# A two-branch kernel on one core: its state-space branch regrouped into units of 64 channels, with other buffers, queues and last steps

## The chip, the core and the metric

The kernel runs on one core of a Trainium2 chip. The core has five engines, each with its own in-order instruction stream: TensorE (PE in the profile, with its weight loads as PEld), VectorE (DVE), ScalarE (ACT), GpSimd (POOL) and SyncE (SP). SP, ACT and POOL issue the transfers between the chip's memory and the on-chip buffers. An instruction that waits holds up everything behind it on its own engine. The metric is the time of one execution in microseconds; lower is better.

## What is computed

Two independent branches, joined along the last axis. Branch A is a Fourier mixing layer, a chain of dense float32 products. Branch B is a state-space layer: a convolution of u with a kernel K of length 2048 for each of 512 channels, where K is a sum over 128 complex exponentials.

```python
# A: x is 1 x 2048 x 512
a = einsum("bsd,ed->bse", x, dft_hid_re); b = einsum("bsd,ed->bse", x, dft_hid_im)
yA = einsum("ts,bse->bte", dft_seq_re, a) - einsum("ts,bse->bte", dft_seq_im, b)
# B: u is 1 x 2048 x 512
A = -exp(log_A_real) + 1j * A_imag;  C = (C_real + 1j * C_imag) * dt;  dt = exp(log_dt)
K = 2 * einsum("dn,dnl->dl", C, exp(A * dt * l)).real            # l = 0..2047
yB = irfft(rfft(u, 4096) * rfft(K, 4096))[:2048] + u * D_skip
out = concatenate([yA, yB], axis=-1)
```

## The kernel before

**The stream (branch A, class Fnet).** Each float32 operand is split into a high part (ACT, L192) and a remainder (DVE, L196, the "split"), and each product becomes three matmuls of 128 x 128 by 128 x 512 (L309). There are 160 rounds of 12 such matmuls, 1920 in all. First eight groups of 16 rounds multiply by the sequence matrices and store intermediate tiles p; then four groups of 8 rounds load p again and give the output ya. Operands come through SP into 4 buffers named raw and 3 pairs named hi and lo; results leave through ACT (L323) into y and through SP.

**The state-space part (branch B, class Ssm).** It runs on the same engines, woven into the stream.
- *Tables.* For chunks of 32 channels, DVE builds two tables of exponentials, t1 and t2, by repeated doubling (prod L541, t L550, L564, L570). ACT makes the seeds (L585 to L603) and squares.
- *Taps.* PE multiplies the two tables of a chunk (L738, one "taps" group per chunk, 16 in all), ACT copies the result to ks. After two chunks (64 channels) a first transform of K runs on PE (L768), ACT evicts it to xk_sb (L779), and POOL stores it to xk in memory (L785).
- *Spectrum of u.* u is loaded in eight pieces (L808, by POOL), transformed (L814), evicted (L824) and stored to xu (L831, by POOL), early in the run.
- *Products.* The spectra are loaded (L878, by POOL) in the units "quarter h of 128 channels, part q of 8 values of s", 4 x 4 products. For each, PE makes a second transform of u and of K (64 matmuls, L907), ACT evicts (L918), DVE multiplies complex numbers in ten operations (L929 to L945), PE makes the first inverse transform (L952), ACT evicts to z (L967), and POOL stores z to zs (L973).
- *Second inverse.* Two steps per quarter load zl from zs (L1000, or L1008 for the last quarter, each part on its own), run 32 matmuls (L1023), and send yb out (L1041 by POOL; L1034 by SP and ACT for the last quarter).

**What sets the order.** The order on every engine is fixed when the program is built. The class Plan keeps a list of ready processes and, at each step, takes the one that can start first on its engine, with an estimate of each operation's length (functions act, dve, load, and fixed figures for PE). A process yields an engine with an estimate and an urgency, or a semaphore (a buffer), or an event. So an estimate does not delay anything on the chip, but it decides in which order the instructions stand. The stream's matmuls have the lowest urgency and fill PE wherever the state-space part is not ready. A first inverse (L952) is joined to the next taps group on PE while taps are left.

**Buffers.** A pool b_two serves the first three quarters with single buffers: one xt_u, one xt_k, one uk, one z, one zl. Beside it lies a pool b_tab with everything of the tables, and with ks and xk_sb. When the last xk has been sent, b_tab is given back and b_last takes its place for the last quarter, with more buffers (xt_k 4, uk 3, z 2). The last quarter's u goes into buffers of b_two that are then idle (L858 to L866).

The functions that the change touches, and their callers, as they stand before:

Of the kernel before, what the change touches and what calls it, by code (L numbers as in the profile page):

```python
# [8 lines left out]
F32 = mybir.dt.float32  # L9
# [8 lines left out]
PART = DM // 4  # L18
# [6 lines left out]
def fft_constants():  # L25
# [27 lines left out]
    ib = np.tile(ib.reshape(4, 8, 2, 32, 32).swapaxes(0, 1).reshape(64, 32, 32), (2, 1, 1))  # L53
# [3 lines left out]
HOP, RESULT, LATENCY = 0.3, 0.15, 3.3  # L57
STREAM = 5
URGENT = (lambda: -0.5),
APART = None, True  # L60
# [14 lines left out]
class Plan:  # L75
# [11 lines left out]
    def step(self, p, value):  # L87
        self.now = p[0]
        while True:
# [15 lines left out]
            else:  # L105
                if r[0] != p[5]:
                    p[0] += HOP
                elif r[0] == "dve" and len(r) < 4:
                    p[0] += RESULT
# [27 lines left out]
    def run(self):  # L137

        while self.ready:
# [10 lines left out]
            p[0] = start + dur + (LATENCY if engine.startswith("dma") else 0.0)  # L150
# [184 lines left out]
class Buffers:  # L335


    def __init__(self, pool, n):
        self.pool, self.n, self.un, self.zn = pool, n, UKS[n - 1], ZS[n - 1]
        self.xts, self.uks, self.zbs = {"u": Sem(n), "k": Sem(n * n)}, Sem(self.un), Sem(self.zn)  # L340
# [21 lines left out]
class Ssm:  # L362


    def __init__(self, tc, ctx, plan, nd, ldt, dsk, uG, f1u, f1k, w2, ia, ib, out):
# [6 lines left out]
        self.xk = dram.tile([4, 2, 32, 2, 32, PART], F32, name="xk")  # L372
        self.zs = dram.tile([4, 2, 8, 4, 2, 32, PART], F32, name="zs")
# [12 lines left out]
        self.zq_ev = [Event() for _ in range(4)]  # L386
        self.xk_ev, self.zs_ev = [Event() for _ in range(4)], [Event() for _ in range(4)]
# [5 lines left out]
    def start(self, pool, done):  # L393
        self.tab, self.tab_ev = pool, done
# [6 lines left out]
        self.quarters()  # L401
# [11 lines left out]
    def banks(self, n):  # L413

        yield self.one
# [36 lines left out]
    def load_tables(self):  # L452
# [7 lines left out]
        par = self.tab.tile([128, 32, 64], F32, name="xk_sb").rearrange("p a b -> p (a b)")  # L460
# [65 lines left out]
    def load_par(self, ck):  # L526
# [4 lines left out]
        yield "dma", load(2 * CHUNK)  # L531
# [173 lines left out]
    def kernels(self):  # L705
        for n in range(8):
            yield self.kss
            ks = self.tab.tile([128, 16, 64], F32, name="ks")
# [11 lines left out]
    def taps(self, ks, n, done):  # L720
# [21 lines left out]
        self.taps_left -= 1  # L742
        if other:
            self.plan.set(other)
# [11 lines left out]
    def stage1_k(self, ks, n, ev):  # L756
# [17 lines left out]
        xs = self.tab.tile([128, 32, 64], F32, name="xk_sb")  # L774
# [6 lines left out]
        xk = self.xk[n // 2].rearrange("b l c s d -> b (c s) l d")[..., 64 * (n % 2):64 * (n % 2) + 64]  # L781
        yield "dma", load(1400)
# [4 lines left out]
        if n % 2:  # L787
            self.plan.set(self.xk_ev[n // 2])
        if n == 7:
            self.plan.set(self.tab_ev)  # L790

    def spectrum_u(self):
# [5 lines left out]
        self.xu_sb, self.xus = b.pool.tile([128, 2, 2, DM], F32, name="zl", bufs=b.n), Sem(2)  # L798
        for k in range(8):
            name = "uk"[k % 2]  # L800
            yield self.sets[0].xts[name]
            self.plan.spawn(self.stage1_u(k, name), 1)

    def stage1_u(self, k, name):
        nc, b = self.nc, self.sets[0]
        u = b.pool.tile([128, 2, DM], F32, name=f"xt_{name}")
        yield "dma", load(512)
        nc.gpsimd.dma_start(u, self.uG[:, 2 * k:2 * k + 2])  # L808
# [7 lines left out]
        self.plan.put(b.xts[name])  # L816
# [11 lines left out]
    def store_u(self, x, m, sem):  # L828
        yield "dma", load(512)
# [9 lines left out]
    def quarters(self):  # L839
# [3 lines left out]
        self.left, self.xt = [4] * 4, {}  # L843
        self.xt_ev = {(n, h, q): Event() for n in "uk" for h in range(4) for q in range(4)}
        xu = [self.xu[..., PART * h:PART * h + PART] for h in range(4)]
        self.plan.spawn(self.spectra("u", xu, [self.xu_ev] * 4), 1)
        self.plan.spawn(self.spectra("k", self.xk, self.xk_ev), 1)
        self.plan.spawn(self.products(), 1)
        for h in range(4):
            self.plan.spawn(self.inverses(h), 1)  # L850
# [270 lines left out]
```

## Time and profile before

| what | value |
|---|---|
| three runs | 609.29, 605.38, 608.88 us; median 608.88 |
| profiled execution | 606.6 us |
| its span, first to last instruction | 604.5 us |
| mean granted PE clock | 0.985 |
| memory traffic | 81.56 MB read, 42.73 MB written, 206 GB/s over the span |
| transfers issued by POOL | 58.47 MB, 35.1% of the 16 DMA engines' time |
| transfers issued by SP | 65.33 MB, 33.6% |

The profile has several views. The page gives busy time per engine and the span in 40 slices of 15.1 us, each digit being tenths of busy time. Windows give busy time of each engine in a stretch of the span, in the order PE, PEld, DVE, ACT, POOL (number of instructions in brackets), then the granted clock, the mean share of the DMA engines and GB/s. The chain that ended last is a list of start, length, engine, tile and line, followed back from the last instruction. A row of waits says which engine's instruction waited for what, the sum in us, how many times and the longest. A row of groups gives line, engine, operation, operands, count, then busy us and mean ns of one, then idle time ahead of it and what ended that. The order of instructions is taken from the built programs and has no times. PE executes each float32 matmul of the state-space part as two instructions, so that 64 matmuls of the order are x128 in the trace.

### The profile page before, as it was taken

To read this page: it belongs to the slowest core of one execution; us is meant where nothing else is said; L and a number is where in the kernel's file an instruction comes from. 1 tells how busy PE (TensorE), PEld (TensorE's weight loads), DVE (VectorE), ACT (ScalarE), POOL (GpSimd) and SP (SyncE) were. 2 spreads that over 40 slices of the span, in tenths; PEclk is the share of its full clock that TensorE was granted. 3 is DMA by queue.
4 is the path that set the end of the run, shared out by engine and by line. 5 is a ranking of instruction groups with operands and counts; after the bars stand their busy time and mean duration, and the time that the engine had idled before them with its cause. 6 is when DMAs were issued, how large, how long until landed. Compare 5 with 4: busy or idle time off the path is not lost.

```text
span 604.5 us, 17668 instructions
## 1 busy us (share of the span) xinstructions
PE 573.6 (95%) x7302; PEld 441.6 (73%) x7302; DVE 536.1 (89%) x948; ACT 380.7 (63%) x743; POOL 125.0 (21%) x186
## 2 busy tenths in 40 slices
PE   6999999999979999999999899999999999999962
PEld 4877677787758877876887778867877777776742
DVE  5999889999979999999999999999999999629620
ACT  4589896867846686558565849495945555435430
POOL 0022333110210131022121222013211312330330
PEclk8999999999999999999999999999999999999986
DMA  8999998463573277536776775367877795897775
GB/s 280 299 288 311 327 324 253 159 159 93 145 232 91 89 210 189 166 94 184 209 237 209 209 197 170 102 197 187 268 249 229 196 260 142 228 311 248 209 218 132
DMA packets 55503, 125.43 MB, mean 207 GB/s; under 512 B 7232, under 2 KB 11712, under 8 KB 55168
## 3 DMA queue, kind: packets, MB, share of 16 engines
q0 software_dynamic: 16672, 58.47, 35.1%
q1 hardware_dynamic: 38080, 65.33, 33.6%
q8 instruction: 57, 0.93, 0.6%
q10 hardware_dynamic: 672, 0.52, 0.3%
q14 instruction: 22, 0.18, 0.1%
HBM read 81.56 MB, written 42.73 MB: 206 GB/s over the span
## 4 chain that ended last, share of the span: by engine, by line
DVE 37%; PE 34%; DMA 11%; issue 9%; ACT 7%; POOL 1%; SPq 0%; POOLq 0%; ACTq 0%; DVEq 0%
PE acc L309 26%; DVE prod L541 12%; DVE lo L196 7%; DVE t L550 7%; PE f L907 3%; DMA xk<-xk_sb 2%; DMA zl<-zs 2%; DMA zs<-z 2%; DMA xt_k<-xk 2%; PE f L1023 2%; PE f L738 2%; PE f L952 2%; DMA raw<-in_sT 2%; DVE t L570 1%; DVE cs L612 1%
## 5 line engine op out<-in xcount | busy, mean ns | idle before, releaser
L309 PE MATMUL acc<-hi,x_hi 128*128 128x512 f32 x640 | 258.4, 404 | 5.6 <-ACT x_hi L192 2.8
L309 PE MATMUL acc<-lo,x_hi 128*128 128x512 f32 x640 | 250.8, 392 | 1.3 <-DVE lo L196 1.3
L309 PE MATMUL acc<-hi,x_lo 128*128 128x512 f32 x640 | 250.0, 391 | 0.0
L541 DVE TENSOR_TENSOR prod<-t,cs 128x1024 f32<-128x1024 f32 (+4 forms) x192 | 165.0, 870 | 4.6 <-ACT t L680 2.6
L309 PEld LDWEIGHTS acc<-hi,x_hi 128*128 128x128 f32 x640 | 120.5, 188 | 53.1 <-issue 19.2
L192 ACT ACTIVATE hi<-raw 128x512 fp32r<-128x512 f32 x160 | 99.5, 628 | 91.6 <-PE acc L309 72.4
L309 PEld LDWEIGHTS acc<-hi,x_lo 128*128 128x128 f32 x640 | 120.6, 188 | 26.4 <-DVE x_lo L196 0.3
L309 PEld LDWEIGHTS acc<-lo,x_hi 128*128 128x128 f32 x640 | 120.8, 189 | 25.4 <-DVE lo L196 2.5
L196 DVE TENSOR_TENSOR lo<-raw,hi 128x512 fp32r<-128x512 f32 x160 | 108.8, 685 | 20.1 <-ACT hi L192 19.9
L550 DVE TENSOR_TENSOR t<-prod 128x512 f32<-128x512 f32 (+3 forms) x192 | 95.0, 512 | 1.3
L557 ACT ACTIVATE square<-t 128x256 f32<-128x256 f32 (+1 forms) x64 | 36.7, 573 | 19.0 <-DVE t L550 11.9
L785 POOL DMA_DIRECT2D xk<-xk_sb x32 | 26.4, 831 | 72.6 <-ACT xk_sb L779 72.6
L918 ACT ACTIVATE uk<-f 128x1024 f32<-128x1024 f32 x32 | 31.7, 1016 | 11.8 <-PE f L907 11.7
L323 ACT ACTIVATE y<-acc 128x512 f32<-128x512 f32 x48 | 28.6, 595 | 14.5 <-PE acc L309 8.4
L973 POOL DMA_DIRECT2D zs<-z x32 | 22.4, 705 | 67.6 <-ACT z L967 61.1
L738 PEld LDWEIGHTS f<-t,t 128*32 128x32 f32 x2048 | 29.4, 110 | 6.9 <-issue 5.0
L738 PE MATMUL f<-t,t 128*32 128x64 f32 x2048 | 32.2, 220 | 0.8 <-issue 0.8
L929 DVE TENSOR_TENSOR z<-uk 128x512 f32<-128x512 f32 x32 | 21.2, 686 | 8.2 <-ACT uk L918 4.5
L617 ACT ACTIVATE cs<-cs 128x352 f32<-128x352 f32 x32 | 15.5, 539 | 17.5 <-DVE cs L612 17.4
L907 PE MATMUL f<-xt_k,w 64*32 64x128 f32 x1088 | 23.1, 271 | 2.7 <-DMA xt_k<-xk 2.5
L570 DVE TENSOR_TENSOR t<-square 128x128 f32<-128x128 f32 (+1 forms) x64 | 24.7, 386 | 0.3 <-ACT square L557 0.3
L1023 PE MATMUL f<-zl,ib 64*32 64x128 f32 x512 | 11.2, 310 | 12.5 <-DMA zl<-zs 12.4
(105 smaller groups left out, 583.0 us busy)
## 6 DMA issues: line engine op xcount, KB each, us to landing
raw<-in_sT SPq DMA_DIRECT2D x127, 256.0 KB, 3.9
p<-y SPq DMA_DIRECT2D x32, 256.0 KB, 4.9
xk<-xk_sb POOLq DMA_DIRECT2D x32, 256.0 KB, 6.1
xt_k<-xk POOLq DMA_DIRECT2D x16, 512.0 KB, 6.4
zs<-z POOLq DMA_DIRECT2D x32, 256.0 KB, 5.0
raw<-p SPq DMA_DIRECT2D x32, 256.0 KB, 3.8
xt_u<-xu POOLq DMA_DIRECT2D x13, 512.0 KB, 6.3
zl<-zs POOLq DMA_DIRECT2D x12, 512.0 KB, 6.3
```

The lines of the kernel that those rows point to most:

```text
L192: self.nc.scalar.activation(hi, src, AF.Copy)
L196: self.nc.vector.tensor_tensor(lo, src, hi.bitcast(F32), op=OP.subtract)
L309: nc.tensor.matmul(acc[d], l[:, cols], r, start=k == 0 and n == 0, stop=k == len(items) - 1 and n == 2)
L323: self.nc.scalar.activation(y, ps, AF.Copy, scale=-1.0 if g[2] == 1 else 1.0)
L541: self.nc.vector.tensor_tensor(p.rearrange("p k d c m -> p k (d c) m"), src.rearrange("p d c l -> p (d c) l")[:, None, :, rows].to_broadca ...
L550: self.nc.vector.tensor_tensor(dst[:, :, :, rows], p[:, 0], p[:, 1, :, ::-1], op=OP.add)
L557: self.nc.scalar.activation(sq, t[:, :, :, m // 2:m], AF.Square)
L570: self.nc.vector.tensor_tensor(t[:, :, 0, m:2 * m:2], box[0][:, :, 0], box[0][:, :, 1], op=OP.subtract)
L738: nc.tensor.matmul(ps[32 * j:32 * j + 32, i], t1[:, d, c], t2[:, d, c], start=c == 0, stop=c == 1, tile_position=(0, 32 * j))
L785: nc.gpsimd.dma_start(xk[k % 2, :, l], xs[64 * (k % 2):64 * (k % 2) + 64, l])
L907: nc.tensor.matmul(got[r][1][32 * xx:32 * xx + 32, g, o:o + PART], self.w2[rows, 8 * q + 4 * r + xx, 32 * c:32 * c + 32], xt[rows, r, xx], ...
L918: a.activation(uk[:, r].rearrange("p g n c d -> p g (n c d)"), p, AF.Copy)
```

## The change

- **Units.** The spectra, products and zs are cut into 8 units of 64 channels with 2 parts of 16 values of s (before 4 quarters of 128 channels with 4 parts of 8). There are 16 products in either kernel, of the same size. u and K of a product now share one tile xt, and a matmul streams 64 columns of u and 64 of K at once. A unit's K is complete after two taps groups, not four.
- **Second inverse.** Units 0 to 5 are taken in pairs, 128 columns as before (new line L1016). Units 6 and 7 have a step of their own each (inverse_alone, L1053): 64 matmuls of 64 columns.
- **Two last steps put behind.** The second step of units 4 and 5, and the step of unit 6, wait in the plan for the event last_ev, which is set when the last first inverse is on PE.
- **Buffers.** ks and xk_sb move to a pool of their own (b_k). b_tab holds the tables alone and is given back at the sixteenth taps group. The last three products' xt and the last four products' uk and z come from b_last (xt 2, uk 2, z 3).
- **Queues.** SP issues the loads of u (new line L816), and for the last unit the store of xk, the loads of xu and xk, the stores of zs and the loads of zl. ACT issues the outputs of yb. POOL keeps the rest.
- **Plan.** POOL's transfers are estimated 1.7 us longer (POOLQ). banks() first yields NOW, which puts the process in the ready list at the present time. While taps are left, DVE's operations of products 11 and later have urgency 3 in place of 1.

The core of the diff (new line numbers; "h" is a unit, "q" a part):

```diff
-PART = DM // 4
+PART, PARTS = DM // 8, 8
+POOLQ = 1.7
+NOW = "now", 0.0
+SLOW = None, False, POOLQ
...
     def taps(self, ks, n, done):
         self.taps_left -= 1
+        if not self.taps_left:
+            self.plan.set(self.tab_ev)
...
     def stage1_k(self, ks, n, ev):
-        for k in range(4):
-            l = slice(16 * (k // 2), 16 * (k // 2) + 16)
-            nc.gpsimd.dma_start(xk[k % 2, :, l], xs[64 * (k % 2):64 * (k % 2) + 64, l])
+        queue, extra = self.queue(n)
+        for b in range(2):
+            queue.dma_start(xk[b], xs[64 * b:64 * b + 64])
...
-        nc.gpsimd.dma_start(u, self.uG[:, 2 * k:2 * k + 2])
+        nc.sync.dma_start(u, self.uG[:, 2 * k:2 * k + 2])
...
+    def queue(self, h):
+        if h < PARTS - 1:
+            return self.nc.gpsimd, SLOW
+        return self.nc.sync, URGENT
...
     def product(self, b, h, q, got, done):
-                            nc.tensor.matmul(got[r][1][32 * xx:32 * xx + 32, g, o:o + PART],
-                                             self.w2[rows, 8 * q + 4 * r + xx, 32 * c:32 * c + 32], xt[rows, r, xx],
+                            nc.tensor.matmul(out[:, :, c, e], self.w2[rows, 16 * q + x, 32 * c:32 * c + 32],
+                                             xt[rows, :, x], start=True, stop=True, tile_position=(64 * g, 32 * xx))
+        late = lambda: 3 if 2 * h + q >= LATE and self.taps_left else 1
...
+        if (h, q) == (PARTS - 1, 1):
+            self.plan.set(self.last_ev)
...
     def inverse(self, h, i):
+        if (h, i) == (2, 1):
+            yield self.last_ev
...
+    def inverse_alone(self, h):
+        if last:
+            for q in range(2):
+                yield self.zq_ev[q]
+                yield "dma", load(600), *URGENT
+                for c in range(2):
+                    nc.sync.dma_start(z[2 * q + c:128:4], zs[q, c])
+        else:
+            yield "dma", load(1024), *SLOW
+            nc.gpsimd.dma_start(z, self.zs[h].rearrange("b s q c l d -> (b s q c) l d"))
+            yield self.last_ev
+        for w in range(8):
+            for j in range(4):
+                for g in range(2):
+                    nc.tensor.matmul(ps[32 * j:32 * j + 32, g, PART * w:PART * w + PART], self.ib[rows, l], z[rows, l],
+                                     start=True, stop=True, tile_position=(64 * g, 32 * j))
...
+            pool_k = ctx.enter_context(tc.tile_pool(name="b_k", bufs=1, side="right"))
             with tc.tile_pool(name="b_tab", bufs=1, side="right") as pool:
-                b.start(pool, tables)
+                b.start(pool, pool_k, tables)
```

Lines of the new kernel that later parts name: the stream L316 (was L309), its split L203 (L196), taps L747 (L738), transform of K L779 (L768) and its store L796 (L785), loads of spectra L887 (L878), products L917 (L907), first inverse L961 (L952), store of zs L985 (L973), second inverse L1016 and L1053 (L1023).

More of the change, by code (lines that the diff above doesn't have):

```diff
@@ L105, in step @@
             else:
+                if r is NOW:
+                    p[4] = r
+                    self.ready.append(p)
+                    return
                 if r[0] != p[5]:
                     p[0] += HOP
-                elif r[0] == "dve" and len(r) < 4:
+                elif r[0] == "dve" and not r[3:]:
                     p[0] += RESULT
@@ L875, in load_spectrum @@
[L875 to L886 removed]
+        for h in range(6, 8):
+            self.plan.spawn(self.inverse_alone(h), 1)
@@ new lines, in load_spectrum, with products @@
+    def load_spectrum(self, n, h, q, x, ev):
+        yield ev
+        queue, extra = self.queue(h)
+        yield "dma", load(512), *extra
+        queue.dma_start(self.xt[h, q][0][:, n], x.rearrange("b l c (q s) d -> q (b l c) s d", q=2)[q])
+        self.plan.set(self.xt_ev[n, h, q])
+    def products(self):
+        for h in range(PARTS):
+            yield self.set_ev[self.set_of(h)]
+            b = self.sets[self.set_of(h)]
+            for q in range(2):
+                for n in range(2):
```

253 lines of the change are left out of this document (115 added, 138 removed).

## The prediction

> **What bounds the kernel now.** I read the page first: the busy shares, then the slices, to see whether one engine is full all the way.
>
> ```profile
> span 604.5 us, 17668 instructions
> PE 573.6 (95%) x7302; PEld 441.6 (73%) x7302; DVE 536.1 (89%) x948; ACT 380.7 (63%) x743; POOL 125.0 (21%) x186
> ...
> PE   6999999999979999999999899999999999999962
> ...
> DVE  5999889999979999999999999999999999629620
> ...
> DMA  8999998463573277536776775367877795897775
> ```
>
> PE is full until the last two slices, and DVE nearly full until slice 34; then DVE falls to 6, 2 and 9. So there are two stretches, and the border is where the tables end. The busy time of four windows (head, DMA-heavy start, middle, end) puts numbers on it; the third ends where PE starts the sixteenth and last group of taps (L738).
>
> ```profile
> 0.00:15.00 15.00, 10.43 (x28) 7.25 (x29) 7.89 (x21) 6.81 (x11) 1.43 (x6) 0.89 0.85 280
> 15.00:101.00 86.00, 86.00 (x578) 63.03 (x576) 79.45 (x154) 70.58 (x146) 23.24 (x39) 1.00 0.94 307
> 101.00:514.70 413.70, 406.05 (x5436) 318.22 (x5434) 404.83 (x710) 269.85 (x534) 77.18 (x106) 1.00 0.63 181
> 514.70:604.50 89.80, 71.13 (x1268) 53.16 (x1267) 43.88 (x67) 33.42 (x54) 23.20 (x35) 0.92 0.75 224
> ```
>
> In the middle window PE is idle for 413.70 - 406.05 = 7.7 us and DVE for 413.70 - 404.83 = 8.9: both are the bound, each waiting a little for the other. In the last window PE is idle for 18.7 of 89.8 us, while DVE works only 43.9. The waits of PE name that idle time, and the chain that ended last shows its steps.
>
> ```profile
> PE f L1023 <- DMA zl<-zs: 12.4, 2, 11.7
> ...
> PE f L907 <- DMA xt_k<-xk: 2.5, 2, 2.1
> ```
>
> ```profile
> 443.56 15.18 PE acc L309 x66
> 458.74 1.15 PE f L1023 x64
> 459.89 2.26 PE acc L309 x9
> 462.15 1.05 PE f L952 x32
> 463.20 1.92 PE f L738 x128
> ...
> 468.77 1.96 PE f L907 x128
> ...
> 514.75 1.92 PE f L738 x128
> ...
> 518.94 1.94 PE f L768 x16
> ...
> 539.01 1.58 PE f L907 x95
> ...
> 580.66 1.16 PE f L952 x32
> 583.21 5.31 DMA zs<-z
> ...
> 591.20 4.26 DMA zl<-zs
> 595.73 3.74 PE f L1023 x128
> 600.12 0.69 DVE zl L1031
> ```
>
> The last matmuls of the Fourier part (L309) are over before the last state-space store goes out. From the end of the last L952 (580.66 + 1.16 = 581.8) to the first L1023 (595.7) 13.9 us pass with 11.7 of them empty on PE: eviction, a store of zs, its landing, a load of zl. Then 64 matmuls at a lowered clock (window 4 grants 0.92 on average): 3.7 us, where the same two steps take 2 x 1.15 elsewhere. From their end (599.4) to the end of the span 5.1 us go to eviction and output.
>
> **The change, part by part.** I took the instruction order of both programs, engine by engine, and priced each stretch by the rows above.
>
> *PE's rates.* (15.18 - 2.26) / 57 = 0.227 us per Fourier matmul, and 2.26 - 9 x 0.227 = 0.22 for each return to that part. A product (L907) 1.96, its first inverse (L952) 1.05, taps 1.92, L768 1.94, a second-inverse step (L1023) 1.15 or less. The order has 1024 product matmuls of 128 columns in either kernel, now u and k together as 2 x 64 out of two places. Two forms of the trace stream 512 columns, L814 from one run and L768 from 16 runs of 32:
>
> ```profile
> L768 PE MATMUL f<-ks,f1k 32*128 32x512 f32 x128 | 16.5, 613 | 0.1
> L814 PE MATMUL f<-xt_u,f1u 32*64 32x512 f32 x64 | 5.4, 613 | 0.0
> ```
>
> Both take 613 ns, so a split operand costs nothing and a product stays at 1.96; a split result in PSUM is not in the trace, and if each half cost what a 64-column matmul of L738 does, a product would be 2 x 1.92 and sixteen of them 30 us dearer. Two rows with splits on the reading side and the equal bytes make me take nothing. Two of the eight final steps become 64 matmuls of 64 columns; nearest is L738, also 64 of 64 columns: 1.92 each against 2 x 1.15 = 2.3 for the two old steps, so +1.5 us.
>
> *PE behind the last taps.* In the new order there stand 225 Fourier matmuls (before 195), the taps, 4 products, 5 first inverses, L768's successor, 2 steps of the old kind, 2 of the 64-column kind, 14 returns: 225 x 0.227 + 1.9 + 4 x 1.96 + 5 x 1.05 + 1.9 + 2 x 1.1 + 2 x 1.9 + 14 x 0.22 = 77.1 us. Before, the same sum is 68.4 us. So 30 matmuls, 6.8 us, moved from ahead of the last taps to behind them, and 15 of them are now the last of the stream, after the last state-space step.
>
> *When the last taps come.* PE alone would reach them 7 us earlier, at 507.7. But they need DVE's tables, and the order says that DVE has 114 product operations and 167 splits ahead of its last table operation, against 110 and 169. The rows are two groups by line, DVE's last table operation in the timeline, and three waits of DVE (the first up to 100 us, the others from 100 to 514):
>
> ```profile
> L929 DVE TENSOR_TENSOR z<-uk 128x512 f32<-128x512 f32 x32 | 21.2, 686 | 8.2 <-ACT uk L918 4.5 <-DMA xt_k<-xk 2.1 <-DMA zs<-z 1.4
> L196 DVE TENSOR_TENSOR lo<-raw,hi 128x512 fp32r<-128x512 f32 x160 | 108.8, 685 | 20.1 <-ACT hi L192 19.9
> ...
> 513.45 0.69 DVE L550 TENSOR_TENSOR t<-prod 128x512 f32<-128x512 f32 x1
> ...
> DVE prod L541 <- ACT t L680: 2.6, 1, 2.6
> DVE z L929 <- ACT uk L918: 2.1, 1, 2.1
> DVE lo L196 <- ACT hi L192: 1.2, 2, 0.7
> ```
>
> That is 2 x 0.69 = 1.4 us more, so DVE cannot be done earlier unless it idles less than the 6.6 us of window 2 and the 8.9 of window 3. The named waits are 2.6 us up to 100 us and 3.3 from there to 514; the rest is gaps of a tenth. The products of a 64-channel unit wait for two groups of taps, not four, so DVE gets products earlier, and PE, being ahead, keeps it waiting less. I take 3.6 of the 5.9 as saved: last taps at 514.7 + 1.4 - 3.6 = 512.5. The ends are 507.7 (PE's own) and 516.1 (nothing saved). The rule that puts late products' DVE work behind the tables is in these counts.
>
> *The end.* The last L961 and the last L1053 stand 24 + 60 Fourier matmuls, one 64-column step and two returns apart: 84 x 0.227 + 1.9 + 0.4 = 21.4 us. The chain under it was 13.9. So PE should not wait, and the 11.7 us go; what is late next is the Fourier part itself. Its last eviction, store and landing take the place of the old tail of 5.1; I take 5.5, since three transfers leave at once. The two steps put behind the last L961 (one of 128 columns, one of 64) are part of that cover or directly behind it.
>
> *Short pieces.* The loads of xu and the stores of zs now run in pieces of 256 bytes, not 512. The stores of xk had 256 already, with the same 256 KB. The rows: the queue that POOL feeds, three kinds of transfer with the median time to landing, a wait of POOL, and one issue on ACT's queue.
>
> ```profile
> q0 software_dynamic: 16672, 58.47, 35.1%
> ...
> xk<-xk_sb POOLq DMA_DIRECT2D x32, 256.0 KB, 6.1
> zs<-z POOLq DMA_DIRECT2D x32, 256.0 KB, 5.0
> xt_u<-xu POOLq DMA_DIRECT2D x13, 512.0 KB, 6.3
> ...
> POOL xt_u L808 <- PE f L814: 31.4, 2, 31.0
> ...
> 600.84 0.40 ACTq L1034 DMA_DIRECT2D out_yb<-zl  x1
> ```
>
> 6.1 against 5.0 prices it: +1.1 per store of 256 KB, and by bytes +2.2 per load. 16.8 MB are concerned; at 212 us of queue time per 58.47 MB that is 61 us, and 22% more is 13 us in 504, 0.03 of the DMA share (0.63 and 0.75 in windows 3 and 4): hidden. A product's load is issued some 25 us before its matmuls, so 2.2 us are hidden too. On the last chain 13.9 + 1.1 = 15.0 is still under 21.4.
> [...]
>
> *Queues.* SP takes over the eight loads of u, the last unit's xk, xu and zs; ACT takes seven outputs of yb more, at the 0.40 us of the row below 2.8 us of an engine that is 63% busy: nothing. POOL has 127 transfers to issue where it had 174 and is 21% busy: nothing. On SP everything behind a waiting transfer waits. The loads of u waited on POOL for PE (31.4 us in the row above); behind them on SP stand loads of raw. At the end nine loads of raw stand behind the wait for the last xk. The order puts 9.75 rounds of 12 matmuls of raw ahead of that, 26 us of work from the last taps on; the chain from L768's end (520.9) to the first L907 of that unit (539.0) took 18.1, and the new order leaves it 66 matmuls, two products, two first inverses and five returns, 22.1. So nothing, and 3 to 8 us if that cover is gone.
> The last units' buffers lie where only the tables lay, and come free at the last taps instead of at the last store of xk: no cost, and xu can land before xk does.
>
> **Sum.** 512.5 + 77.1 + 1.4 (before: 18.7 - 11.7 - 5.1 = 1.9 of small waits in the last window, xt_k among them) + 5.5 = 596.5 us, 8.0 less than 604.5. The profiled execution took 606.6, 2.1 more than its span: 598.6. The four executions shown (609.29, 605.38, 608.88, 606.6) average 607.5, and the median of three is 608.88, 2.3 above the profiled one; I take the 8.0 off the mean: 599.5.
>
> **Rivals.**
> 1. *PE's order holds as it is, DVE is no bound.* Last taps at 507.7, the rest as above: 4.8 us less, 594.7. For it: PE waited for DVE by name hardly at all before. Against: it needs DVE to lose 516.1 - 507.7 = 8.4 us of the 15.5 that it idles in windows 2 and 3, and only 5.9 of them have a name. Chance 0.20.
> 2. *DVE saves nothing and the end does not fit.* Last taps at 516.1 or a little later, or the chain of the last unit overruns its cover by 4 us: 603 to 608. This is the case in which the change does not do what it says: the empty time moves from the last step to the taps. Chance 0.20.
> 3. *SP holds back the raw loads: slower.* In window 2 DMA is at 0.94 and PE has no idle time, so loads of raw come just in time. If each of the six loads of u that must wait for an earlier L814 holds SP, PE starves. It cancels the gain at 8.0 / 6 = 1.3 us for each and makes it slower by over 1% at (8.0 + 6.1) / 6 = 2.4; at 3 us, 617. Against: three to seven other loads stand between most of them, and raw has four buffers and three split ones ahead. Chance 0.08.
> The forecast itself 0.52.
>
> **Chances.** 1% is 6.1 us, about what a measurement of this kernel can tell from no change. The forecast is faster by 8.0, so part of its own spread lies within 1%: of 0.52 I count 0.44 as faster, 0.08 as within; rival 1 is faster, rival 2 within, rival 3 slower. Faster 0.64, same 0.28, slower 0.08. Range: from rival 1 with a shorter tail (592) to rival 2's upper end (608); outside lie rival 3 and about a tenth below and above.
>
> **What would show it.** PE's wait for zl<-zs should be gone or under 2 us. The last taps should start at 508 to 516, with PE's idle time ahead of them some 5 us above before's 7.7, named after DVE or the splits. L917 should take 1.96 per product and L1053 1.9. The last instruction on PE should be a Fourier matmul, at full clock, about 5.5 us before the end. The landing of zs and xu should be 1 to 2 us longer. Wrong would be: a wait for raw before 100 us, L917 above 2.1, or a gap ahead of the last L1053.

## The result, and the profile after

The changed kernel takes 630.86 us (median of 4 runs, 628.84 to 635.14); before took 608.5 beside it (4 runs, 605.38 to 609.29). The ratio is 1.039 (95% interval 1.032 to 1.045): slower by 22 us, where 8 us less had been forecast. A median here is over all executions of a kernel; a ratio is worked out apart, without those more than 1.5% above its fastest, and the two can differ by half a per cent or so. The profiled execution took 629.86 us, with a span of 628.1.

From the page: the span, the busy time, and the slices of PE, DVE and PE's granted clock.

```profile
span 628.1 us, 17885 instructions
PE 584.6 (93%) x7430; PEld 448.2 (71%) x7430; DVE 536.1 (85%) x947; ACT 381.9 (61%) x744; POOL 120.8 (19%) x139
...
PE   8999999799789998998969979999898899979996
...
DVE  6999999899599997999969959989799999757620
...
PEclk9999999899989998999989998999999999999998
```

DVE is busy for the same 536.1 us as before. PE's hole before the last slices is gone, and small holes have come in the middle: slices of 6 and 7 on PE, of 5, 6 and 7 on DVE. The windows of before, taken again (the last two cut at before's last taps):

```profile
0.00:15.00 15.00, 13.42 (x46) 9.90 (x47) 9.95 (x25) 7.60 (x12) 0.21 (x4) 1.00 0.86 252
15.00:101.00 86.00, 84.87 (x695) 62.24 (x697) 83.95 (x159) 73.01 (x157) 20.76 (x34) 1.00 0.93 314
101.00:514.70 413.70, 382.22 (x5037) 296.28 (x5030) 374.90 (x656) 253.72 (x498) 89.44 (x86) 0.97 0.64 169
514.70:628.10 113.40, 104.13 (x1660) 79.74 (x1658) 67.29 (x110) 47.60 (x80) 10.35 (x15) 0.99 0.79 218
```

Up to 101 us little is wrong. From there to 514.7 PE idles 31.5 us (before 7.7) and DVE 38.8 (before 8.9). The sixteenth taps group (L747) starts at 540.88 us, not 512.5. One window each from 0 to the start of the last taps, first before, then after:

```profile
0.00:514.68 514.68, 502.46 (x6035) 388.47 (x6035) 492.18 (x881) 347.22 (x690) 101.84 (x151) 1.00 0.69 205
```

```profile
0.00:540.88 540.88, 506.68 (x6005) 389.81 (x6005) 494.94 (x885) 345.25 (x686) 110.97 (x125) 0.98 0.69 195
```

DVE's work ahead of the last taps is 494.94 us, 2.8 more than before (1.4 was forecast). Its idle time there is 540.88 - 494.94 = 45.9 us, where before it was 22.5. So the 26.2 us are 2.8 of work and 23.4 of waiting. The waits, of DVE, then of ACT, and last the one wait of ACT for raw from in_sT in before:

```profile
DVE lo L203 <- ACT hi L199: 47.4, 25, 7.6
DVE z L938 <- DMA zs<-z: 6.6, 1, 6.6
DVE z L938 <- ACT hi L199: 6.5, 1, 6.5
```

```profile
ACT hi L199 <- DMA raw<-in_sT: 14.5, 8, 6.5
ACT y L330 <- DMA p<-y: 8.6, 3, 3.9
...
ACT hi L199 <- DMA raw<-p: 7.6, 2, 6.2
```

```profile
ACT hi L192 <- DMA raw<-in_sT: 11.5, 6, 3.7
```

The split (L203) waits for ACT's high part, and ACT waits for raw to land (14.5 + 7.6 = 22.1 us; before 11.5) and for a buffer y whose store p is late (8.6 us). PE's waits:

```profile
PE acc L316 <- ACT y L330: 9.1, 5, 3.3
PE f L917 <- issue: 9.0, 4, 3.8
PE acc L316 <- DVE lo L203: 8.4, 7, 3.3
PE f L747 <- issue: 5.3, 5, 1.3
PE f L747 <- DVE t L559: 3.7, 2, 1.9
```

There is no wait for zl<-zs any more. "issue", 14.5 us in all, is a wait for nothing that the profile names. Counting PE's instructions in the trace (a weight load and a matmul are two, and PE's own waits for semaphores count) shows where: each such wait stands at a count of 192 to 194 more than a multiple of 256, and one of the 58 packets of 16384 bytes on the queue named "instruction" ends 1.2 to 1.6 us before PE goes on. So I read that PE's instructions come in pieces of 256, and that a dense group (L917: 256 instructions in 1.96 us) uses a piece up before the next is there.

Three suspects could be seen in this trace. **A:** POOL's small addition (L772) is held. This is the timeline of POOL:

```profile
151.98 9.70 POOL L772 TENSOR_TENSOR ks<-dskip,ks 128x16 f32<-128x16 f32 x1 [19.76 <-ACT ks L759]
161.62 1.67 POOL L985 DMA_DIRECT2D zs<-z  x2
```

An addition of 16 columns takes 9.70 us (another takes 8.8, the other six at most 1.0); the stores of zs behind it on POOL go out late, and DVE waits 6.6 and 6.5 us for the one buffer z (the second is put down to ACT, but it ends at 369.72 us, 0.1 after the store has landed). While it is held, DVE is busy for 9.60 of the 9.70 us (8.66 of 8.75 in the other), and all but one of its operations there (L602, 0.34 us) have two on-chip inputs. Either addition ends 0.09 us after the last of them, where DVE falls idle (6.6 and 6.5 us). But DVE is busy for 0.84 or more of the time beside the six short ones too, and beside before's eight, which take 0.23 to 0.74 us. So the trace shows two additions that are held; that DVE's operations hold them is my reading.
**C:** the late stores of p. **E:** PE's instruction pieces.

### The profile page after: what moved, and what is told of

Same layout as the page of the kernel before. It is cut to its first block, busy times and chain, and to the rows that moved or that the text cites. A ratio compares the mean times of both kernels' runs of the same rounds, so it can differ in the third digit from the quotient of the medians.

```text
span 628.1 us, 17885 instructions
## 1 busy us (share of the span) xinstructions
PE 584.6 (93%) x7430; PEld 448.2 (71%) x7430; DVE 536.1 (85%) x947; ACT 381.9 (61%) x744; POOL 120.8 (19%) x139
## 3 DMA queue, kind: packets, MB, share of 16 engines
q0 software_dynamic: 13104, 45.88, 30.2%
## 4 chain that ended last, share of the span: by engine, by line
PE 37%; issue 4%; DVE 4%; DMA 4%; ACT 2%; ACTq 0%; DVEq 0%; POOLq 0%
PE acc L316 28%; PE f L917 3%; PE f L747 2%; DMA raw<-in_sT 2%; PE f L961 2%; DMA raw<-in_wT 1%; PE f L779 1%; DVE prod L550 1%; DMA xt<-xk 1%; PE f L1016 1%; DVE lo L203 1%; DVE t L559 1%; ACT hi L199 0%; PE f L1053 0%; ACT L608 0%
## 5 line engine op out<-in xcount | busy, mean ns | idle before, releaser
L316 PE MATMUL acc<-hi,x_hi 128*128 128x512 f32 x640 | 261.6, 409 | 9.1 <-ACT y L330 9.1
L316 PE MATMUL acc<-lo,x_hi 128*128 128x512 f32 x640 | 255.2, 399 | 8.4 <-DVE lo L203 8.4
L316 PE MATMUL acc<-hi,x_lo 128*128 128x512 f32 x640 | 253.8, 397 | 0.0
L316 PEld LDWEIGHTS acc<-hi,x_hi 128*128 128x128 f32 x640 | 122.8, 192 | 57.0 <-issue 18.9
L203 DVE TENSOR_TENSOR lo<-raw,hi 128x512 fp32r<-128x512 f32 x160 | 109.4, 687 | 47.8 <-ACT hi L199 47.4
L316 PEld LDWEIGHTS acc<-lo,x_hi 128*128 128x128 f32 x640 | 122.7, 192 | 36.2 <-DVE lo L203 12.5
L316 PEld LDWEIGHTS acc<-hi,x_lo 128*128 128x128 f32 x640 | 122.6, 192 | 26.8 <-DVE x_lo L203 0.3
L559 DVE TENSOR_TENSOR t<-prod 128x512 f32<-128x512 f32 (+4 forms) x192 | 95.7, 513 | 1.1
L917 PE MATMUL f<-xt,w 64*32 64x128 f32 x2048 | 35.0, 274 | 9.6 <-issue 9.0
L566 ACT ACTIVATE square<-t 128x256 f32<-128x256 f32 (+1 forms) x64 | 36.5, 571 | 11.2 <-DVE t L559 9.7
L747 PE MATMUL f<-t,t 128*32 128x64 f32 x2048 | 33.7, 220 | 9.0 <-issue 5.3
L747 PEld LDWEIGHTS f<-t,t 128*32 128x32 f32 x2048 | 29.9, 110 | 16.1 <-issue 10.2
L772 POOL TENSOR_TENSOR ks<-dskip,ks 128x16 f32<-128x16 f32 x8 | 22.2, 2774 | 98.9 <-ACT ks L759 98.9
L917 PEld LDWEIGHTS f<-xt,w 64*32 64x32 f32 x2048 | 29.2, 106 | 16.7 <-issue 13.8
L926 ACT ACTIVATE uk<-f 128x1024 f32<-128x1024 f32 x32 | 31.8, 1014 | 13.8 <-PE f L917 12.0
L985 POOL DMA_DIRECT2D zs<-z x28 | 23.5, 844 | 57.3 <-ACT z L978 57.2
L841 POOL DMA_DIRECT2D xu<-zl x22 | 13.4, 612 | 66.6 <-ACT zl L834 65.5
```

The lines of the kernel that those rows point to most:

```text
L203: self.nc.vector.tensor_tensor(lo, src, hi.bitcast(F32), op=OP.subtract)
L316: nc.tensor.matmul(acc[d], l[:, cols], r, start=k == 0 and n == 0, stop=k == len(items) - 1 and n == 2)
L559: self.nc.vector.tensor_tensor(dst[:, :, :, rows], p[:, 0], p[:, 1, :, ::-1], op=OP.add)
L566: self.nc.scalar.activation(sq, t[:, :, :, m // 2:m], AF.Square)
L747: nc.tensor.matmul(ps[32 * j:32 * j + 32, i], t1[:, d, c], t2[:, d, c], start=c == 0, stop=c == 1, tile_position=(0, 32 * j))
L772: nc.gpsimd.tensor_tensor(ks[:, :, 0], self.dskip[:, 16 * n:16 * n + 16], ks[:, :, 0], op=OP.add)
```

## The experiments

Times below are medians; each ratio is against runs of before on the same chip, and kernels that ran on different chips compare better by their ratios. "Idle" is DVE's idle time ahead of the last taps, by a window as above; "raw" is ACT's waits for raw from in_sT and p together.

| run | kernel | us | ratio (95%) | last taps | idle | raw |
|---|---|---|---|---|---|---|
| before | | 608.5 | 1 | 514.7 | 22.5 | 11.5 |
| after | | 630.9 | 1.039 (1.032-1.045) | 540.9 | 45.9 | 22.1 |
| e1 | after, A repaired | 620.6 | 1.015 (1.008-1.022) | 528.6 | 32.0 | 22.2 |
| e2 | after, one more y | 626.0 | 1.022 (1.015-1.029) | 534.4 | 40.0 | 31.8 |
| e3 | e1 and e2 | 617.1 | 1.010 (1.003-1.017) | 524.2 | 28.4 | 30.2 |
| e4 | before, with e1's edit | 613.0 | 1.005 (1.001-1.008) | 521.8 | 28.1 | 11.3 |
| e5 | e3, pieces shifted by 176 | 611.1 | 1.000 (0.996-1.004) | 520.6 | 25.0 | 31.9 |
| e6 | before, shifted by 128 | 616.4 | 1.013 (1.007-1.018) | 523.0 | 29.2 | 13.8 |
| e7 | e3, planner as it was | 617.9 | 1.014 (1.009-1.020) | 532.7 | 31.8 | 12.1 |
| e8 | e3, queues as they were | 616.6 | 1.013 (1.007-1.018) | 524.0 | 28.3 | 29.3 |
| e9 | e5 again | 610.5 | 1.002 (0.998-1.005) | 524.4 | 29.0 | 26.3 |
| e10 | e3 again | 616.3 | 1.008 (1.004-1.012) | 530.8 | 35.2 | 28.5 |
| e11 | e3, POOLQ 3.4, shifted | 599.8 | 0.986 (0.981-0.991) | 513.5 | 20.5 | 3.0 |
| e12 | e3, L961 apart, shifted | 616.0 | 1.013 (1.008-1.019) | 513.4 | 18.8 | 13.7 |
| e13 | e3, POOLQ 3.4 | 600.3 | 0.983 (0.975-0.990) | 514.4 | 21.4 | 2.5 |
| e14 | after, POOLQ 3.4 | 611.5 | 1.002 (0.998-1.006) | 523.4 | 28.1 | 1.8 |
| e15 | e3, POOLQ 2.6, shifted | 599.1 | 0.980 (0.974-0.986) | 514.6 | 20.6 | 5.0 |
| e16 | e3, half of xk stored | 603.5 | 0.988 (0.983-0.992) | 513.4 | 18.5 | 19.2 |
| e17 | control of e16 | 617.0 | 1.008 (1.003-1.014) | 521.5 | 26.8 | 39.3 |
| e18 | e13, half of xk stored | 603.6 | 0.990 (0.983-0.997) | 514.3 | 21.3 | 3.5 |

The last three columns come from one profiled execution each: the longest of its kernel's runs, or the next to it, in e4, e5, e9 and e10 (614.9, 616.8, 618.8 and 622.7 us), one of the shortest in e3, e7, e8 and e17 (613.1, 615.6, 611.3 and 610.9).

### A and C: the addition on POOL, and one more buffer y (e1 to e4)

```diff
-nc.gpsimd.tensor_tensor(ks[:, :, 0], ...)        # L772
+nc.vector.tensor_tensor(ks[:, :, 0], ...)        # e1, e3; in before: e4
-name="y", bufs=STAGED
+name="y", bufs=STAGED + 1                        # e2, e3
```

> The changed kernel with one edit: the addition of D_skip to ks (L772) is emitted on DVE, not on POOL, at the same place of the order; every other instruction keeps its place. Theory A (POOL's addition is held while DVE works without a gap: 9.7 us at 152 and 8.8 us at 355, and the stores of zs behind it on POOL hold DVE's products): the two waits of DVE of 6.6 and 6.5 us and PE's waits after them (about 9 us) go, the last taps start at 525 to 532 instead of 540.9, and the time is 615 to 622. Rival B (POOL's long span is only how the profile draws it, and DVE waits for PE and the loads anyway): the waits move elsewhere, last taps above 537, time within 4 us of 630.9.

> The changed kernel with a fourth buffer for y (name y, STAGED + 1), the plan and the order unchanged. Theory C (stores of p that take 8 to 10 us to land beside POOL's transfers hold y, so ACT cannot evict and PE waits 9.1 us in 5 waits, after which its clock is low for some us): the waits of PE for ACT y go, and 8 to 12 us of the time with them, 619 to 623. Rival B (DVE's work sets the taps, PE only waits in another place): PE's waits for y go, but its waits for DVE and for the tables grow by as much; time within 3 us of 630.9.

> Both edits of the two runs before it: addition on DVE, four buffers for y. If both theories hold and the losses add, 606 to 613, with the last taps at 517 to 524; the instruction-fetch waits of PE (14.5 us called issue) stay. If one loss hides behind the other, it equals the better of the two runs alone.

> The kernel before with the same addition on DVE. Its POOL additions took 0.23 to 0.74 us each, so theory A expects nothing: within 2 us of before. If moving the addition gains 5 us or more here too, the gain has another reason than the two long holds.

On DVE the eight additions cost 1.5 us. DVE's waits for the store of zs are gone from e1, which is 10.2 us faster than after by the medians and 2.4%, some 14 us, by the ratios: A is shown, with a size of 10 to 14 us. In before, where the same addition is never held (0.23 to 0.74 us each), the edit gains nothing (e4, 3.6 us slower where at most 2 were expected; why is open). One more buffer y took PE's waits for y from 9.1 us to 1.6; it gave 4.9 us by the medians and 1.7%, some 10 us, by the ratios (e2), but only 3 to 3.5 on top of e1 (e3); the time of e2, 626.0, stays above the 619 to 623 that the theory wanted. Both together leave 617.1, still 8 us above before.

### E: where PE's instruction pieces end (e5, e6, e9, e10)

```diff
-for n in range(3):  matmul(ps[:, :256], z[:, :128], z[:, 256:])
+for n in range(47): matmul(ps[:32, :8], z[:, :32], z[:, 256:264])   # e5, e9; 35 in e6
```

> The kernel of e3 with its three wide warming matmuls at the start (256 columns) replaced by 47 narrow ones (8 columns, 32 rows of result), so that PE's instruction stream is 176 slots longer ahead of the work; the order of everything else is the same on every engine. Theory E (PE's instructions come in pieces of 256 slots, and a piece that is used up in under some 4 us is followed by a wait for the next): in e3's trace the sum of what pieces fall short of 4 us is 22.4 us, and with the boundaries 176 slots on it is 14.7. PE's waits named issue (11.0 us in e3) should fall to 4 to 7, and the time from 617.1 to 608 to 613. Rival (these waits hide others, or do not hang on the place in the stream): waits named issue 9 to 12 at the same groups, time within 2 us of e3.

> The kernel before with its three warming matmuls replaced by 35 narrow ones: 128 slots more ahead of the work, order otherwise unchanged. Theory E: the sum of what pieces fall short of 4 us goes from 18.9 to 29.1 us in the trace of before, so the waits named issue rise from 2.3 us to some 8 to 12 and the time by 4 to 10 us (613 to 619). Rival (before is free of these waits for another reason, its order or its queues): no change within 2 us.

> The kernel of e5 once more, beside e10 on the same chip: in e5 the profiled execution was the longest of ten (616.8 at a median of 611.1) and its waits named issue were 11.0 us, as in e3, so the time met theory E's expectation and the waits did not. Theory E: waits named issue 4 to 8 us in an execution near the median, time 4 to 9 us under e10's. Rival (the gain of e5 came from elsewhere, the start or the chip): within 2 us of e10.

> The kernel of e3 unchanged (three wide warming matmuls, no shift), as the partner of e9. It has 2.0 us less of warming matmuls at the start than e9 (PE's first matmul of the stream at 4.7 against 6.7 us). Theory E: waits named issue some 11 us, time 4 to 9 us above e9's in spite of the earlier start. Rival: within 2 us of e9, or faster than it.

In the order of e3 the place counts: e9 is 5.8 us under e10 by the medians and 0.6%, some 4 us, by the ratios (12 runs each, same chip), although it starts some 2 us later. e6 is 6.3 us slower than before, of which the start is 0.7, and its waits named issue are 7.3 us in all, where before has 2.3. PE's waits named issue in e9, then in e10:

```profile
PE acc L316 <- issue: 3.2, 2, 2.9
PE f L917 <- issue: 2.9, 2, 2.4
PE f L1016 <- issue: 2.2, 1, 2.2
PE f L747 <- issue: 1.8, 1, 1.8
```

```profile
PE f L917 <- issue: 10.3, 4, 4.3
PE f L747 <- issue: 5.5, 4, 3.1
```

10.1 against 15.8: the difference fits the time, though these two executions, each the longest of its twelve, are 3.9 us apart, and the sum in e9 stays above the 4 to 8 that were expected. In e5 it was 11.0, no less than in e3. So the effect is there, but my count of short pieces does not foretell its size. It rested on 4 us as the time that a piece must last, an assumption that no trace had shown, and that of after does not bear it out: six of its ten waits follow pieces that PE used up in 1.5 to 3.0 us, four follow pieces of 4.2 to 5.6, and four pieces of 1.9 to 3.9 us were followed by no wait. The count failed for other orders too: e12 had the smallest shortfall and 12.4 us of such waits, and for e13 see below.

### The plan and the queues undone (e7, e8)

```diff
-POOLQ = 1.7 ... yield NOW ... LATE = 11
+POOLQ = 0.0 ...               LATE = 99        # e7
-return self.nc.sync, URGENT                    # and u, zl on SP, yb on ACT
+return self.nc.gpsimd, ...                     # e8: all of them on POOL
```

> The kernel of e3 with the planner as it was: no longer estimate for POOL's transfers, no NOW in banks, no lower urgency for DVE's late products. The work is the same, the order of it is not. If the new order cost time ahead of the last taps (the products too early on DVE or too late), this is faster than e3 by 4 us or more, with the last taps ahead of 520. If the order is what brings DVE's work forward, it is slower by 4 us or more. Theory E alone expects the sum of waits named issue to change with the order, in a direction not known: time within 5 us of e3.

> The kernel of e3 with every transfer back on POOL that the change moved to SP and ACT (loads of u, the last unit's xk, xu, xk, zs and zl, outputs of yb); the order on PE and DVE is unchanged. Rival 3 of the prediction (SP holds back raw): faster than e3 by 3 us or more, the waits of DVE for hi and of PE for lo smaller. Theory: SP was no cost, so it is no faster; the last transfers go through a POOL that also issues the outputs, 1 to 4 us slower at the end. Time 615 to 622.

e8 takes as long as e3 (616.6 and 617.1 us), and its waits for raw are as long: the transfers on SP and ACT are not the cause in e3's order, and rival 3 falls. The end did not get slower either. e7 came out even, in another way than either expectation: the wait for the last zl came back (11.0 us), and the last taps came at 532.7. So the planner's three edits together did their work at the end; e7 does not tell them apart. The size of the estimate was the next thing to try.

### A longer estimate, and the first inverse apart (e11 to e15)

```diff
-POOLQ = 1.7
+POOLQ = 3.4        # e11, e13, e14; 2.6 in e15
-if self.taps_left > 1:
+if self.taps_left > 99:        # e12: L961 never joined to the taps
```

> The kernel of e3 with the planner's extra for POOL's transfers raised from 1.7 to 3.4 us, so that the products stand later in the order, and 39 narrow warming matmuls, the shift at which this order has few short pieces by a count over its instruction order (the shortfall below 4 us is 6.2 us of that count, where e3's order has 10.1 and e5's 7.7). If the waits of L917 for xk (4.2 us in e3, 6.3 in e5) come from an estimate that is too short, they fall under 2 us and the time is 2 to 6 us under e9's, which would be faster than before. If the order cannot hide it, the wait goes over to DVE, and the time is e9's or more.

> The kernel of e3 with the first inverse (L961, 64 slots) never joined to a taps group (L747, 256 slots), and 15 narrow warming matmuls, the shift at which this order has few short pieces (shortfall 3.5 us by the same count). Theory E: the five waits of L747 named issue (4.1 us in e3) go to under 1.5 us in sum; against it stand some ten more returns to the stream at 0.22 us, 2.2 us. Time 608 to 613. Rival: the waits move to other groups, time as e10.

> The kernel of e11 without its shift (the three wide warming matmuls back): only the longer estimate of 3.4 us for POOL's transfers is left, beside e3's two repairs. If the order is what made e11 faster (products later, no wait for xk, DVE always with work at hand), the time stays at 600 to 604. Theory E: this place in the stream has many short pieces (shortfall 15.5 us by the count over the order, 6.2 in e11), so waits named issue rise from 6.7 us to over 10 and the time to 606 to 614.

> The changed kernel itself with one constant edited, POOLQ from 1.7 to 3.4: ks is still added on POOL and y has its three buffers. If the loss of the change lay in the order that too short an estimate gives, this is within 6 us of before (603 to 615). If POOL's held addition and the late stores of y cost what e1 and e2 showed (10 and 5 us) whatever the order is, it is some 15 us above e13.

> e3's kernel with 2.6 us in place of 1.7 and the shift of e9 (shortfall 7.3 us by the count over the order). e11 ended with PE waiting 6.9 us for the last zl, because its order leaves less of the stream behind the last taps. If the estimate moves work from one side of the last taps to the other in steps, 2.6 keeps more of the cover: wait for zl under 3 us, last taps at 513 to 518, time 597 to 604. If the order at 2.6 is as e3's, the waits for xk come back (over 3 us) and the time is 606 to 612.

The constant changes no instruction, only their order. With it e3's kernel goes from 617.1 to 600.3 (e13), with or without the shift (e11 599.8), and that is 1.7% faster than before. The window up to the last taps and two waits of PE in e13:

```profile
0.00:514.35 514.35, 508.39 (x6065) 395.10 (x6066) 492.96 (x889) 349.34 (x695) 89.48 (x118) 1.00 0.73 209
```

```profile
PE f L1053 <- DMA zl<-zs: 8.0, 1, 8.0
PE f L747 <- issue: 2.1, 3, 1.0
```

PE idles 6.0 us ahead of the last taps. The waits for instructions are small (5.8 us in all) at a place in the stream where I had expected over 10: theory E's expectation failed. e14 shows that the constant alone takes the changed kernel from 630.9 to 611.5; against e13, on the same chip, A and C cost 11.2 us in that order too. e15 at 2.6 has no wait for the last zl and takes 599.1 us, not clearly apart from e11 and e13; what its shift adds was not tried apart. e12 missed: its last taps come at 513.4, but its order has 258 matmuls of the stream behind them (225 in after), PE idles 14 us there, and the gain ahead is lost behind.

What does the order do? The last column of the table goes with it: ACT waits 22 to 30 us for raw in after, e3 and e8, and 2 to 5 in e11, e13, e14 and e15. It is not the whole of it: e7 has 12.1 us in this column and still 31.8 of idle time on DVE. In after the late loads come in bursts. Here is one of them, the transfers issued from 437 to 450 us, with the median time to landing last:

```profile
xk<-xk_sb POOLq DMA_DIRECT2D x2, 512.0 KB, 9.6
raw<-in_sT SPq DMA_DIRECT2D x3, 256.0 KB, 10.0
out_yb<-zl ACTq DMA_DIRECT2D x1, 512.0 KB, 12.5
p<-y SPq DMA_DIRECT2D x1, 256.0 KB, 11.4
```

The same row over the whole run:

```profile
raw<-in_sT SPq DMA_DIRECT2D x127, 256.0 KB, 4.0
```

A load of raw takes 4.0 us in the median of the whole run, here 10.0. From 101 us to 514.7, 11 of after's 111 loads of raw take over 8 us to land, 1 of 123 in before and 4 of 124 in e13. Theory **D**: K's store to xk (1 MB) goes out together with a group's four stores of p. When they are issued in after, by POOL and by SP:

```profile
230.05 2.19 POOL L796 DMA_DIRECT2D xk<-xk_sb  x2 [6.20 <-ACT xk_sb L790]
300.00 2.18 POOL L796 DMA_DIRECT2D xk<-xk_sb  x2 [6.62 <-ACT xk_sb L790]
375.98 2.17 POOL L796 DMA_DIRECT2D xk<-xk_sb  x2 [9.86 <-ACT xk_sb L790]
437.18 2.17 POOL L796 DMA_DIRECT2D xk<-xk_sb  x2 [7.47 <-ACT xk_sb L790]
```

```profile
234.06 0.33 SPq L335 DMA_DIRECT2D p<-y  x1
...
300.20 4.54 SPq L335 DMA_DIRECT2D p<-y  x3
...
371.42 1.41 SPq L335 DMA_DIRECT2D p<-y  x3
...
435.32 4.13 SPq L335 DMA_DIRECT2D p<-y  x3
```

And in e13:

```profile
239.12 2.20 POOL L796 DMA_DIRECT2D xk<-xk_sb  x2 [6.21 <-ACT xk_sb L790]
295.67 2.22 POOL L796 DMA_DIRECT2D xk<-xk_sb  x2 [5.52 <-ACT xk_sb L790]
```

```profile
216.07 2.23 SPq L335 DMA_DIRECT2D p<-y  x3
...
272.84 2.03 SPq L335 DMA_DIRECT2D p<-y  x3
```

In after all of the first six stores of xk (106 to 437 us) are issued ahead of a group's four stores of p, by 5 us at most, or among them; in before three of six, in e15 one, in e13 none, where they follow some 9 us or more behind the last. ACT's waits for raw stand in the same order: 22.1, 11.5, 5.0 and 2.5 us. So far that is an argument; the next three runs test it.

### D: the store of xk halved (e16 to e18)

```diff
-for b in range(2): queue.dma_start(xk[b], xs[64 * b:64 * b + 64])
+for b in range(1): ...                         # e16, e18; e17 keeps 2
-queue.dma_start(xt[:, n], x...)                # n = 1, K's spectrum
+queue.dma_start(xt[:64, n], x[0]...); queue.dma_start(xt[64:, n], xu[1]...)
```

e16 to e18 leave out half of K's spectrum, so they show times alone and are no versions to use.

> The kernel of e3 with half of each store of xk left out (512 KB instead of 1 MB; the second half of the rows is not stored) and the load of K's spectrum taking its second half from xu instead, as two transfers of the same bytes in sum; so the taps' transform is used only in half. The order on PE, DVE, ACT and SP is e3's. Theory D (in this order the 1 MB store of xk goes out just ahead of the four stores of p, and raw loads issued behind them land 8 to 11 us after issue in place of 4; ACT waits for raw, DVE for ACT, and the tables come late): ACT's waits for raw fall from 30 us in e3 to under 15, DVE's idle time ahead of the last taps from 28 to 24 or less, the time to 604 to 611, at least 5 us under e17's. Theory of distance and fetch alone: within 3 us of e17.

> The control of e16: the loads as in e16 (half of K's spectrum from xu), but the whole of xk is stored. The same part of the result is left out. Either theory: waits for raw and time as in e3, 614 to 621 (some us more if the extra transfer of each load costs POOL time).

> The kernel of e13 (POOL's estimate at 3.4, no shift) with the loads and the half store of e16. In e13's order the stores of xk go out behind the stores of p and ACT waits only 2.5 us for raw, so theory D expects little to gain: within 3 us of e13's 600.3. If the bytes of the store cost time in any order (through the DMA engines or POOL), it gains here what e16 gains over e17.

e16 is 13.5 us under its control e17 by the medians and 2.0%, some 12 us, by the ratios; order and chip are the same. In e13's order the halved store gains nothing: e18 is 3.3 us above e13, just outside the 3 that were expected. It has one transfer more for each load of K's spectrum and no control of its own, but in e3's order these transfers cost nothing that shows (e17 617.0, e3 617.1). So it is not the bytes alone but the meeting of the transfers. The windows up to the last taps and ACT's waits, of e16:

```profile
0.00:513.44 513.44, 499.21 (x6006) 384.61 (x6006) 494.98 (x892) 344.16 (x686) 92.24 (x124) 1.00 0.72 198
```

```profile
ACT hi L199 <- DMA raw<-in_sT: 10.0, 5, 3.6
```

and of e17:

```profile
0.00:521.50 521.50, 499.34 (x6005) 383.32 (x6005) 494.74 (x892) 344.18 (x686) 100.14 (x131) 1.00 0.75 202
```

```profile
ACT hi L199 <- DMA raw<-in_sT: 29.9, 13, 6.5
```

DVE's work is the same; its idle time falls from 26.8 to 18.5, and the last taps come at 513.4. The waits for raw were to fall under 15 and fell from 39.3 to 19.2 in all, since those for raw<-p stay at 9.2 (9.4 in e17). The loads themselves show it: from 101 us to 513.4, 25 of e17's 117 loads of raw take over 8 us to land, and 5 of e16's 120. D is shown in e3's order, at 12 to 13.5 us; in the order of after, with A and C in place, it was not tried by itself.

## Why the prediction was wrong

**The failing step is "When the last taps come".** It said that 64-channel units give DVE its products earlier, so that DVE loses 3.6 us of idle time, and bounded the step at 516.1, "nothing saved". DVE's idle time rose by 23.4 us instead. The bound had left out a loss. I had seen that both engines are the bound and wait for each other; then a late transfer at any place (DVE's first wait above counts 25) holds up both, and such a loss has no ceiling near zero. The runs show what stood there in its place: an addition on POOL that is held (A, 10 to 14 us), late stores of p (C, 3 to 10), waits for instructions (E, 14.5 in PE's rows against 2.3) and stores of K that meet the stores of p (D, 12 to 13.5 in e3's order). For D the order was at hand. All of the first six 1 MB stores of K now meet the stores of p, where three did before: the first transform of K (L779) stands 9 to 45 matmuls of the stream ahead of a group's end each time, and before (L768) it stood 21 to 57 ahead four times and 165 twice. I did not lay the two queues beside each other in time.

**"Short pieces ... hidden"** was wrong in its way of judging: 0.03 more of a mean DMA share of 0.63 is nothing, but within a burst the loads behind it land 6 us late, and ACT's waits for raw show that raw has no such cover in the middle of the run. The pieces that went from 512 to 256 bytes show no cost of their own. The row of xk against that of zs had priced them at 22%, but the landing of zs and of the loads of xu, forecast 1 to 2 us longer, is as it was: 6.4 us for xu (6.3 before) and, for zs, 5.0 as before:

```profile
zs<-z POOLq DMA_DIRECT2D x28, 256.0 KB, 5.0
```

**"POOL is 21% busy: nothing"** priced POOL by its busy time; its addition was held for 9.7 us with stores queued behind it (10 to 14 us, e1).

**Right:** the end. The wait for zl went, and the chain was covered. PE ends at 622.6 us (the last row of its chain, below), 81.7 us from the last taps, where 77.1 + 1.4 had been put down; 3.5 of it are two waits for instructions at L917, so without them it is 78.2. The tail is 5.5, as forecast. From the chain that ended last and the groups of after:

```profile
573.45 1.96 PE f L917 x128
...
618.93 3.65 PE acc L316 x15
```

```profile
L1053 PE MATMUL f<-zl,ib 64*32 64x64 f32 x128 | 1.5, 225 | 0.0
```

A product stays at 1.96 where PE isn't kept waiting, and a 64-column step (L1053) costs 1.5, not 1.92: the row it was priced by was too dear. With the order mended (e13) or the burst halved (e16) the last taps come at 514.4 and 513.4, where 512.5 was forecast, and the kernel at 600.3 and 603.5 stands near the 599.5. That is in part chance: both have A and C mended, which the changed kernel has not, e13 waits 8.0 us for the last zl where the forecast had no wait, and e16 leaves out work.

**The rivals.** Rival 3 had the right sign and the right symptom (raw comes late) at the wrong place: not SP in window 2 (e8), but loads of raw that land late from 101 us on (11 of 111 over 8 us, before 1 of 123). Rivals 1 and 2 did not come to pass.

**What stays open.** Why a shift of the instruction pieces is worth 4 to 6 us in e3's order and nothing in e13's; the trace lists the packets that carry them (58 in after, 0.95 MB) among the core's DMA packets, so the bursts may delay them as well, but that was not tried. How much of the 17 us that the longer estimate is worth comes from D and how much from other changes of the order was not measured apart. The parts do not simply add: A 10 to 14, C 3 to 10, shift 4 to 6, D 12 to 13.5 and order 17 were each measured in the presence of some of the others, so they are not to be added up to the 22 us.

## What to carry to other kernels

When two engines are both the bound, price an edit that only moves instructions by the transfers that it brings together: lay the big stores of each queue beside the just-in-time loads, stage by stage, and do not go by the mean DMA share. Bound such a step above as well as below. Where a planner fixes the order, an estimate that is too short (here 1.7 us in place of 2.6 or 3.4 for one queue) can cost more than the change gains, so vary it before judging the change.

## What the runs showed of the hardware

- A POOL operation of 128 x 16 with two on-chip inputs, 0.2 to 1.0 us otherwise in before and after, took 9.70 and 8.75 us in after. DVE was busy for 9.60 and 8.66 us of them, and for 0.84 or more of the time beside the others too.
- PE's waits that the profile names issue stand only at places that are 256 instructions apart (counted in before, after, e3, e9, e10 and e13), in after at ten of 58 such places: up to 3.8 us there and 4.3 in e10, 2.3 us in all in before and 14.5 in after.
- Loads of 256 KB that land after 4.0 us in the median took 10.0 us in after from 437 to 450 us, beside a store of 1 MB and 0.75 MB of other stores.
- PE's granted clock fell after some of its idle times: ahead of the last taps after has six stretches at 0.5, 23.9 us in all, each behind an idle time of PE of 1.9 to 3.8 us, whatever PE waited for; an idle time of 2.97 us at 561.5 was followed by none. e3 has 6.8 us of such stretches. Half of the difference, 8.5 us, is close to the 8.3 us by which the same 6005 instructions of PE are busy longer in after (506.7 us) than in e3 (498.4).
